# Block sums for the query products on GpSimd instead of VectorE

## The chip, the cores and the metric

The kernel runs on one core of a Trainium2 chip. A core has a matrix engine (TensorE, PE in the profile; its weight loads are listed apart as PEld), a vector engine (VectorE, DVE), a scalar engine (ScalarE, ACT), a programmable engine (GpSimd, POOL), and SyncE (SP), which here only issues DMAs. Every engine works through its own instruction stream in order, and waits on semaphores for the others. The metric is the time of one execution on the device, in microseconds.

## The reference

The inputs are `x` (2048 tokens of 512), key and value caches of 32 heads (2048 keys of 128), and weight matrices. All are bf16.

```
xn = layernorm(x)
q  = xn @ wq                                   # 2048 x 4096: 32 heads of 128
p  = softmax(q k^T / sqrt(128));  s = (p v) @ wo
h  = gelu(layernorm(xn) @ w1), its four quarters shifted by 1, -1, 2, -2 tokens
x1 = xn + h @ w2
g  = silu(x1 + gelu(layernorm(x1) @ w3) @ w4)
out = x + s * g
```

## The kernel before

**Stages.** The kernel first normalises the tokens, transposes them into `xnT` (features on the partitions, tokens along the free dimension), and runs most of the gated feed-forward part. From about 125 us it runs attention, with the rest of the feed-forward products mixed in up to about 191 us. Attention is one long loop over 128 units. A unit is one head and one block of 512 queries. Units go by groups of four heads, inside a group by the four query blocks, and inside a block by the four heads. A unit has 8 slots (`SPU`). In each slot TensorE makes the scores of 256 keys (`s_slot`), ScalarE exponentiates them into `pT` (line 436), and TensorE multiplies an earlier unit's `pT` by the values (`pv_run`, ten slots behind). Into the slots are woven the query projection of units to come, and the output projection of units that are done (`wo_slot`).

**VectorE's part in a unit.** It adds up the exponentials for the softmax's denominators: `add_first` (line 442), twice `add_next` (line 447), then `fold` (line 451) and `fold_last` (line 455). All of these read two tiles in SBUF. The sums are transposed by a DMA (`turn`), reduced (line 485), inverted (line 491), and spread by two more DMAs to `rb`. Then `norm` (line 509) scales the attention output from PSUM into `oT`. Lines 559 (first group) and 571 take the output projection out of its single PSUM bank (tag `xm`), which TensorE needs again for the next four products.

**The query projection.** Up to unit 15 the query tiles come from plain products of `xnT` and a head's weights. From unit 16 on, two heads at a time are projected with seven block products instead of eight (Strassen's scheme in Winograd's form). A pair's product is seen as 2 x 2 blocks: 256 tokens by 256 features, and 256 features by one head's 128 columns. The scheme needs sums of blocks:

- `x_sum(qt, i)`, line 356: four sums for each of the four query blocks, of 128 x 512 elements, made once (16 instructions). Sum 2 is written over a block of `xnT` itself, save for the last query block.
- `w_sum(h, i)`, line 365: four sums for each pair of heads from head 4 on, of 128 x 256 elements (14 pairs, 56 instructions). They lie in a tile `wc` with two buffers, so that a pair's sums can be written when the last product of the pair before the previous one has been read.

`product(v, k)` issues the seven products into one PSUM bank (tag `xa`). `q_take` (ScalarE, line 405) and `q_part` (VectorE, lines 413, 416, 418 and 421) combine them into the query tiles. Two of the products write into a half that `q_part` 1 and 2 (lines 416 and 418) must have read before.

**What sets the order.** The order is written out by hand: each instruction is pinned to program order on its engine, and `at(slot, fn)` places work at a slot. The token sums stand one per unit at slot 5 of units 10 to 25. The weight sums of a pair stand at slots 2 and 6 of two units, 4 or 2 units ahead of their group's (units 12 to 15, then every 16 units). The weights of a group's heads are loaded by SyncE's queue (`load_w`, line 164) in units 9 and 12 of the group before. The sums' tiles come from the pool `pS`, which opens in the place of the feed-forward's pool when the last feed-forward product has been issued.

```
for qt in range(QT):
    for i in range(4):
        at((10 + 4 * qt + i) * SPU + 5, lambda qt=qt, i=i: x_sum(qt, i))
for h in range(HG, H, 2):
    u = (h // HG) * QT * HG + (-4, -2)[h % HG // 2]
    for i in range(4):
        at((u + i // 2) * SPU + (2, 6)[i % 2], lambda h=h, i=i: w_sum(h, i))
```

GpSimd computes only some small operations for the layer norms (lines 194 and 205), all of them in the first 54 us.

Of the kernel before, what the change touches and what calls it, by code (L numbers as in the profile page):

```python
# [9 lines left out]
ALU = mybir.AluOpType  # L10
# [7 lines left out]
def kernel(  # L18
# [15 lines left out]
    nc = tc.nc  # L34
# [27 lines left out]
    pin = tc.keep_in_program_order  # L62
# [48 lines left out]
    def mm(out, lhsT, rhs, start, stop, **kw):  # L111
# [9 lines left out]
        out=ident[:], in0=diag[:], scalar1=0.0, scalar2=None, op0=ALU.is_equal))  # L121
# [219 lines left out]
    def x_block(qt, half, dcs):  # L341
        c = qt * 512 + 256 * half
        return xnT[:, dcs, c:c + 256]

    def x_sum(qt, i):
        if i == 2 and qt < QT - 1:
            out = x_block(qt, 1, LO)
        else:
            out = pS.tile([P, 2, 256], BF16, tag="xs", bufs=XS, name="xs")[:]
        a, b, op = (  # L350
            (x_block(qt, 1, LO), x_block(qt, 1, HI), ALU.add),
            (xs.get((qt, 0)), x_block(qt, 0, LO), ALU.subtract),
            (x_block(qt, 0, LO), x_block(qt, 1, LO), ALU.subtract),
            (x_block(qt, 0, HI), xs.get((qt, 1)), ALU.subtract),
        )[i]
        pin(nc.vector.tensor_tensor(out=out, in0=a, in1=b, op=op))
        xs[qt, i] = out

    def w_sum(h, i):
        if i == 0:  # L360
            wc[h] = pS.tile([P, 4, 2, Dh], BF16, tag="wc", bufs=2, name="wc")
        w, o = wc[h], [wc[h][:, k] for k in range(4)]
        b11, b12, b21, b22 = (wqs[h + j][:, d, :] for d in (LO, HI) for j in (0, 1))
        a, b = ((b12, b11), (b22, o[0]), (b22, b12), (b21, o[1]))[i]
        pin(nc.vector.tensor_tensor(out=o[i], in0=a, in1=b, op=ALU.subtract))

    def product(v, k):
        g, qt, hh = units[v]
# [313 lines left out]
    for jc in range(DC):  # L682
        b = BASE_J[jc]
# [153 lines left out]
    for g in range(NG - 1):  # L837
        b = (g * QT + QT - 1) * HG
# [62 lines left out]
    for v in pairs:  # L901
        a = (v - 2) * SPU
# [16 lines left out]
# [7 lines that stand above are left out]
# [108 lines left out]
    def pv_to(k):  # L1034
# [29 lines left out]
        out=diag[:], in0=diag[:], scalar1=0.0, scalar2=None, op0=ALU.is_equal))  # L1064
# [98 lines left out]
```

## Time and profile before

| what | value |
|---|---|
| median of 3 runs | 1236.7 us (1235.96 to 1236.73) |
| the profiled execution's own time | 1236.42 us |
| its span | 1234.6 us |
| TensorE busy | 1227.5 us (99%) |
| ScalarE busy | 1105.8 us (90%) |
| VectorE busy | 1030.1 us (83%) |
| GpSimd busy | 26.6 us (2%) |

The profile is of one execution. Busy time is the time in which an engine's instructions ran. The chain is the work that ended last, followed back from the last instruction to what released it. The waits tell how long an engine sat idle in front of an instruction, and which instruction of another engine released it, as total, number of times, and longest. A row of the timeline gives the start, the duration, the engine, the line, the operation, and the tiles (output, then inputs), with the idle time ahead of it and its releaser in brackets. A row by stretches gives the stretch, its length, the busy time and number of instructions, the granted clock of TensorE, the DMA share and the GB/s.

### The profile page before, as it was taken

How to read it: one execution, taken by the hardware profiler on the slowest of the kernel's cores; microseconds unless marked ns; L12 is line 12 of the kernel's file. 1: busy time of each engine (PE TensorE's matmuls, PEld its weight loads, DVE VectorE, ACT ScalarE, POOL GpSimd, SP SyncE). 2: the span in 40 equal slices, each digit the busy share in tenths (PEclk: the TensorE clock that was granted, in tenths of full speed). 3: DMA queues.
4: the chain of work that ended last, by engine and by line, in shares of the span. 5: the costliest groups of instructions: out<-in, count | busy, mean ns of one | idle time of the engine just before them, and what ended most of it. 6: DMA issues, size and time to landing. Idle time of an engine off the chain costs nothing.

```text
span 1234.6 us, 17534 instructions
## 1 busy us (share of the span) xinstructions
PE 1227.5 (99%) x6267; PEld 636.5 (52%) x6267; DVE 1030.1 (83%) x1647; ACT 1105.8 (90%) x1237; POOL 26.6 (2%) x75
## 2 busy tenths in 40 slices
PE   9999999999999999999999999999999999999998
PEld 6444444455555555555555555555555555555545
DVE  7712778899888888988889888888889999999997
ACT  6345999899999999999999999999999999999996
POOL 5300000000000000000000000000000000000000
PEclk9999999999999999999999999999999999999999
DMA  8661122664334423354243523543345424553342
GB/s 176 168 140 35 31 39 65 96 99 94 63 80 100 106 57 82 87 111 85 58 95 91 111 56 69 103 104 72 76 83 111 107 58 90 99 107 66 77 81 66
DMA packets 244056, 107.75 MB, mean 87 GB/s; under 512 B 194816, under 2 KB 227712, under 8 KB 243968
## 3 DMA queue, kind: packets, MB, share of 16 engines
q1 hardware_dynamic: 243408, 106.17, 41.5%
q8 instruction: 49, 0.80, 0.3%
q10 hardware_dynamic: 560, 0.46, 0.1%
q14 instruction: 39, 0.32, 0.1%
HBM read 67.50 MB, written 2.36 MB: 57 GB/s over the span
## 4 chain that ended last, share of the span: by engine, by line
PE 94%; DVE 3%; DMA 2%; ACT 1%; issue 0%; SPq 0%; DVEq 0%; ACTq 0%
PE ps_s L112 39%; PE ps_o L112 37%; PE ps_wo L112 8%; PE ps_q L112 8%; PE ps_m L112 2%; DMA tT<-acc 1%; DVE acc L447 1%; ACT pT L436 1%; DMA rb<-dr 0%; DMA xin<-in_A_x_dram 0%; DVE sm L485 0%; PE ps_oh L112 0%; DVE oT L509 0%; DVE acc L451 0%; DVE y L1025 0%
## 5 line engine op out<-in xcount | busy, mean ns | idle before, releaser
L436 ACT ACTIVATE pT<-ps_s 128x1024 bf16<-128x1024 f32 x1016 | 1016.2, 1025 | 56.8 <-PE ps_s L112 26.1
L112 PE MATMUL ps_s<-qT,kT 128*128 128x512 bf16 (+1 forms) x2064 | 609.3, 378 | 0.0
L112 PE MATMUL ps_o<-pT,vb 128*128 128x512 bf16 x1984 | 590.2, 379 | 0.0
L447 DVE TENSOR_TENSOR acc<-acc,pT 128x2048 bf16<-128x2048 bf16 x254 | 307.0, 1208 | 54.9 <-ACT pT L436 54.4
L112 PEld LDWEIGHTS <-kT 128*128 128x128 bf16 x2064 | 232.7, 113 | 151.3 <-issue 1.0
L112 PEld LDWEIGHTS <-vb 128*128 128x128 bf16 x1984 | 193.9, 98 | 216.6
L442 DVE TENSOR_TENSOR acc<-pT 128x2048 bf16<-128x2048 bf16 x127 | 155.4, 1224 | 38.4 <-ACT pT L436 35.5
L112 PE MATMUL ps_wo<-wo_h,oT 128*128 128x512 bf16 x496 | 186.3, 379 | 0.0
L451 DVE TENSOR_TENSOR acc<-acc 128x1024 bf16<-128x1024 bf16 x127 | 87.4, 688 | 2.5
L509 DVE TENSOR_TENSOR oT<-ps_o,rb 128x512 bf16<-128x512 f32 x127 | 86.6, 682 | 1.1 <-DMA rb<-dr 0.8
L485 DVE TENSOR_REDUCE sm<-tT 128x4 f32<-128x512 bf16 x124 | 83.9, 676 | 2.8 <-DMA tT<-acc 2.7
L112 PEld LDWEIGHTS <-oT 128*128 128x128 bf16 x528 | 51.4, 98 | 52.6 <-issue 0.6
L112 PEld LDWEIGHTS <-wc 128*128 128x128 bf16 x440 | 43.0, 98 | 54.1 <-issue 2.7
L571 DVE TENSOR_TENSOR sacc<-ps_wo,sacc 128x512 f32<-128x512 f32 x96 | 65.7, 684 | 0.0
L112 PEld LDWEIGHTS <-wq_h 128*128 128x128 bf16 x398 | 38.9, 98 | 46.3
L112 PE MATMUL ps_q<-xnT,wq_h 128*128 128x256 bf16 (+1 forms) x288 | 61.1, 298 | 0.4 <-DVE sacc L559 0.4
L421 DVE TENSOR_TENSOR qT<-ps_q,tq 128x512 bf16<-128x512 f32 x55 | 38.0, 692 | 23.3 <-PE ps_q L112 22.9
L455 DVE TENSOR_TENSOR acc<-acc 128x512 bf16<-128x512 bf16 x127 | 52.9, 417 | 0.5
L293 ACT ACTIVATE h2T<-ps_s 128x1024 bf16<-128x1024 f32 x28 | 28.6, 1023 | 25.9 <-PE ps_s L112 25.9
L112 PE MATMUL ps_s<-xn2T,w_sb 128*128 128x512 bf16 x224 | 48.8, 379 | 0.0
L112 PEld LDWEIGHTS <-w_sb 128*128 128x128 bf16 x368 | 33.5, 98 | 29.6
L112 PE MATMUL ps_q<-xs,wc 128*128 128x256 bf16 x246 | 47.0, 273 | 0.0
(102 smaller groups left out, 585.6 us busy)
## 6 DMA issues: line engine op xcount, KB each, us to landing
rb<-dr SPq DMA_DIRECT2D x127, 256.0 KB, 3.9
vb<-in_A_v_cache_dram SPq DMA_DIRECT2D x62, 256.0 KB, 3.0
wq_h<-in_A_wq_dram SPq DMA_DIRECT2D x32, 128.0 KB, 3.0
wo_h<-in_A_wo_dram SPq DMA_DIRECT2D x32, 128.0 KB, 2.5
w_sb<-in_B_w_dram SPq DMA_DIRECT2D x8, 256.0 KB, 5.0
kT<-in_A_k_cache_dram SPq DMA_TRANSPOSE x128, 2.8
xl<-in_A_x_dram SPq DMA_DIRECT2D x16, 128.0 KB, 3.0
dr<-rc SPq DMA_DIRECT2D x127, 2.0 KB, 1.4
```

What stands on the lines that cost most here:

```text
L112: pin(nc.tensor.matmul(out=out, lhsT=lhsT, rhs=rhs, start=start, stop=stop, **kw))
L293: pin(nc.scalar.activation(out=h2[c, f][:], in_=ps[:], func=ACT.Gelu_apprx_tanh))
L421: pin(nc.vector.tensor_tensor(out=s["q"][:, 1:3], in0=ps, in1=u.to_broadcast([P, 2] + list(u.shape[2:])), op=ALU.add))
L436: pin(nc.scalar.activation(out=s["pT"][-1][:, jj:jj + 2, :], in_=sps[:], func=ACT.Exp, scale=SCALE))
L442: pin(nc.vector.tensor_tensor(out=s["acc"][:], in0=s["pT"][0][:], in1=s["pT"][1][:], op=ALU.add))
L447: pin(nc.vector.tensor_tensor(out=a[:], in0=a[:], in1=st[u]["pT"][i][:], op=ALU.add))
L451: pin(nc.vector.tensor_tensor(out=a[:, 0:2, :], in0=a[:, 0:2, :], in1=a[:, 2:4, :], op=ALU.add))
L455: pin(nc.vector.tensor_tensor(out=a[:, 0, :], in0=a[:, 0, :], in1=a[:, 1, :], op=ALU.add))
L485: pin(nc.vector.tensor_reduce(out=sm[:], in_=s["tT"][:], axis=mybir.AxisListType.X, op=ALU.add))
L509: pin(nc.vector.tensor_tensor(out=to, in0=o, in1=rb, op=ALU.mult))
L571: pin(nc.vector.tensor_tensor(out=sa, in0=ps[:], in1=sa, op=ALU.add))
```

## The change

The two instructions that compute the block sums, `x_sum` and `w_sum`, are issued on GpSimd in place of VectorE. Their places in the program, tiles, operands and operations are the same. All other instructions are the same, and the order on TensorE and ScalarE is too; where TensorE waited for VectorE's sums, it waits for GpSimd's.

```
@@ def x_sum(qt, i):
-        pin(nc.vector.tensor_tensor(out=out, in0=a, in1=b, op=op))
+        pin(nc.gpsimd.tensor_tensor(out=out, in0=a, in1=b, op=op))
@@ def w_sum(h, i):
-        pin(nc.vector.tensor_tensor(out=o[i], in0=a, in1=b, op=ALU.subtract))
+        pin(nc.gpsimd.tensor_tensor(out=o[i], in0=a, in1=b, op=ALU.subtract))
```

## The prediction

> **What bounds the kernel now.** I read the page first (busy times, then the chain), next the waits of TensorE and VectorE, last the timeline beside the moved instructions.
>
> ```profile
> span 1234.6 us, 17534 instructions
> PE 1227.5 (99%) x6267; PEld 636.5 (52%) x6267; DVE 1030.1 (83%) x1647; ACT 1105.8 (90%) x1237; POOL 26.6 (2%) x75
> ...
> PE 94%; DVE 3%; DMA 2%; ACT 1%; issue 0%; SPq 0%; DVEq 0%; ACTq 0%
> ```
>
> TensorE (PE) is busy for 99% of the span and carries 94% of the chain that ended last. VectorE (DVE) is busy 83%, and GpSimd (POOL) 2%. So time that VectorE saves counts only where TensorE waits for it:
>
> ```profile
> PE ps_q L112 <- DVE qT L418: 1.4, 3, 1.0
> PE ps_q L112 <- DVE sacc L559: 0.4, 1, 0.4
> ```
>
> TensorE's waits for VectorE in the attention loop come to 1.4 + 0.4 us. VectorE follows TensorE with a margin, and the question is how large that is and what the new work on GpSimd does to it.
>
> **What is removed.** Grouped by line over the whole span, the 16 token sums (L356), then the 56 weight sums (L365):
>
> ```profile
> 0.00:1235.00 1235.00, 6.69 (x16) 1.00 0.42 87
> 0.00:1235.00 1235.00, 15.96 (x56) 1.00 0.42 87
> ```
>
> That is 6.69/16 = 0.42 us for a token sum and 15.96/56 = 0.285 us for a weight sum, 22.7 us in all. None of it lies on TensorE's path. The largest of the three waits shows why:
>
> ```profile
> 1057.50 0.29 DVE L365 TENSOR_TENSOR wc<-wq_h,wc 128x256 bf16<-128x256 bf16 x1
> 1060.30 0.69 DVE L485 TENSOR_REDUCE sm<-tT 128x4 f32<-128x512 bf16 x1 [1.32 <-DMA tT<-acc]
> 1064.23 0.38 PE L112 MATMUL ps_q<-xnT,wc 128*128 128x256 bf16 x2 [0.98 <-DVE qT L418]
> ```
>
> A weight sum stands ahead of it, but between the two VectorE waits 1.32 us for a DMA, so an earlier weight sum only lengthens that wait. I take the gain as 0, with 1.4 us as its upper end.
>
> **What is added: durations on GpSimd.** GpSimd has no such instruction before, so I bound it by its own rows (ns min/median/max, or busy and mean):
>
> ```profile
> L205 POOL TENSOR_SCALAR ve<-mv x30: 221/222/352, 6.1 to 53.3; 128x1 f32<-128x1 f32 x30
> L118 POOL IOTA diag<- 128x128 f32 x1 | 0.2, 242 | 0.4 <-POOLq L1147 0.4
> L1147 POOL MEMSET const-float32-0.0<- 128x1 f32 x1 | 0.1, 99 | 0.2 <-issue 0.2
> ```
>
> An operation on one element takes 0.22 us. The iota writes 128 elements in 242 ns against 99 ns for one, so about 1.1 ns per element of one stream. One stream's rate as the lower end: 0.22 + 512 x 1.1 ns = 0.79 us for a token sum and 0.50 for a weight sum. Two inputs fetched one after the other as the upper end: 1.35 and 0.79. No row separates them; I take the middle, 1.07 and 0.64, some 2.4 times VectorE's. (The Trainium skill, GPSIMD Engine Reference, section Elementwise — side-by-side cycle accounting, gives 4497 ns for 2048 fp32 elements; by its rate a token sum would be an estimated 1.12 us and a weight sum 0.56. No run here shows that yet.)
>
> **When they run.** GpSimd has nothing else to do after the layer norms, so the sums no longer run at VectorE's places (a token sum in each unit of 8 slots, from 217 to 347 us) but as soon as their data are there, in the order of the program. The pool of the sums opens when TensorE has read the last of the feed-forward tiles, and two token sums go at once. Then the first weight sum of heads 4 and 5 waits for its weights, and later that of heads 6 and 7 holds up the 15 instructions behind it (3 weight sums, 12 token sums):
>
> ```profile
> 191.04 0.38 PE L112 MATMUL ps_m<-w_sb,h2T 128*128 128x512 bf16 x1
> 207.13 1.12 SPq L164 DMA_DIRECT2D wq_h<-in_A_wq_dram  x2
> 236.02 0.39 SPq L164 DMA_DIRECT2D wq_h<-in_A_wq_dram  x1
> wq_h<-in_A_wq_dram SPq DMA_DIRECT2D x32, 128.0 KB, 3.0
> ```
>
> With 3.0 us from issue to landing, heads 4 and 5's weights are there at 207.13 + 1.12 + 3.0 = 211.3 us, and heads 6 and 7's at 236.02 + 0.39 + 3.0 = 239.4. At 211 us a short batch runs (4 weight and 2 token sums), and at 239 a burst starts: 4 x 0.64 + 12 x 1.07 = 15.4 us of GpSimd work, end to end, which before was spread out to 347 us. From head 8 on there are 12 batches of four weight sums, each released by TensorE's last read of the buffer.
>
> Being late is no danger. The first product that reads a combined weight comes at 249.6 us, and its sums (heads 4 and 5) start some 38 us sooner:
>
> ```profile
> L112 PE MATMUL ps_q<-xs,wc x246: 272/273/273, 249.6 to 1181.1; 128*128 128x256 bf16 x123
> ```
>
> **Contention, the term that decides.** The one place before where a GpSimd instruction is plainly lengthened beside VectorE is at 53 us:
>
> ```profile
> 51.94 0.57 POOL L194 TENSOR_TENSOR rs<-ve,nhalf 128x1 f32<-128x1 f32 x1
> 52.79 0.74 POOL L194 TENSOR_TENSOR rs<-ve,nhalf 128x1 f32<-128x1 f32 x1
> 53.65 0.58 POOL L194 TENSOR_TENSOR rs<-ve,nhalf 128x1 f32<-128x1 f32 x1
> 52.79 2.64 DVE L219 TENSOR_SCALAR xn<-xall,mv,rs 128x512 bf16<-128x512 bf16 x8
> ```
>
> The same GpSimd instruction takes 0.57 us ahead of the eight VectorE operations and 0.74 at their start, but 0.58 in their midst; the eight go at 2.64/8 = 0.33 us each. This is weak evidence that the engines hinder each other, in one direction, with a GpSimd operand of one element. Two ends: GpSimd gives way and VectorE is undisturbed (cost 0), or each holds the other off for whole instructions, turn about. I take the second, since the sums read 256 or 512 elements where this one reads one, and a resource that can stop GpSimd must be held by GpSimd when it comes first. (The Trainium skill, SBUF — State Buffer, section Who interferes with whom, states more than the row: a VectorE instruction with two SBUF inputs contends with a GpSimd instruction that reads SBUF, and whichever starts first holds the interface to its end. By that rule, with its durations above, the estimate is +5.6 us; by the row alone, which shows only GpSimd delayed, 0.)
>
> The VectorE instructions that would take turns are those with two SBUF inputs: L442, L447, L451, L455. In the burst they stand so before:
>
> ```profile
> 240.01 1.20 DVE L447 TENSOR_TENSOR acc<-acc,pT 128x2048 bf16<-128x2048 bf16 x1
> 241.24 0.69 DVE L451 TENSOR_TENSOR acc<-acc 128x1024 bf16<-128x1024 bf16 x1
> 241.96 0.43 DVE L455 TENSOR_TENSOR acc<-acc 128x512 bf16<-128x512 bf16 x1
> 242.51 1.22 DVE L442 TENSOR_TENSOR acc<-pT 128x2048 bf16<-128x2048 bf16 x1
> 244.77 1.23 DVE L447 TENSOR_TENSOR acc<-acc,pT 128x2048 bf16<-128x2048 bf16 x1 [0.71 <-ACT pT L436]
> ...
> 249.25 1.20 DVE L447 TENSOR_TENSOR acc<-acc,pT 128x2048 bf16<-128x2048 bf16 x1
> ...
> 254.97 0.68 DVE L559 COPY sacc<-ps_wo 128x512 f32<-128x512 f32 x1
> ...
> 259.02 0.42 DVE L418 TENSOR_TENSOR qT<-ps_q,tq 128x256 bf16<-128x256 f32 x1
> 256.05 0.38 PE L112 MATMUL ps_wo<-wo_h,oT 128*128 128x512 bf16 x1
> 260.37 0.38 PE L112 MATMUL ps_q<-xnT,wc 128*128 128x256 bf16 x2
> ```
>
> Turn about, with VectorE's own sums taken out: L447 240.0 to 241.2, token sum to 242.3, L451 to 243.0, weight sum to 243.6, L455 to 244.1, weight sum to 244.7, L442 to 245.9, token sum to 247.0, L447 to 248.2 (246.0 before). Over the next 2.6 us VectorE reads PSUM or one input, and GpSimd does three sums freely. Then L447 251.0 to 252.2, token sum 253.3, L451 254.0, token sum 255.0, L455 255.5, token sum 256.5, L442 257.7, token sum 258.8, L447 to 260.0. L559 ends at 260.7 instead of 255.65, and L418 at 265.5 instead of 259.44. TensorE needs L559 for its product at 256.05, a margin of 0.40 us, and L418 for that at 260.37, a margin of 0.93. The losses are 5.06 - 0.40 = 4.7 us and 6.05 - 0.93 = 5.1 us; being of one lag they don't add, and the larger counts: **+5.1 us**. With the lower durations the same steps give +2.7, with the upper +8.9, and then the short batch near 211 us may add what one token sum holds VectorE beyond the margin, 1.35 - 0.40 = 1.0: +9.9. With the middle durations I put it at 0: its six sums mostly fall beside VectorE work on PSUM.
>
> A later batch, turn about (before, around the release at 636.2 us):
>
> ```profile
> 635.71 1.23 DVE L442 TENSOR_TENSOR acc<-pT 128x2048 bf16<-128x2048 bf16 x1 [0.54 <-ACT pT L436]
> 638.08 1.21 DVE L447 TENSOR_TENSOR acc<-acc,pT 128x2048 bf16<-128x2048 bf16 x1
> 639.21 0.68 DVE L571 TENSOR_TENSOR sacc<-ps_wo,sacc 128x512 f32<-128x512 f32 x1
> 641.15 0.38 PE L112 MATMUL ps_wo<-wo_h,oT 128*128 128x512 bf16 x1
> ```
>
> L442 ends at 636.94, two weight sums fill the gap to 638.2, L447 starts 0.16 us late (0.44 with the upper duration), and the other two sums run beside L571 and its followers. The margin from L571's end (639.89) to TensorE's product at 641.15 is 1.26 us. Cost 0 for each of the 12; what hides it is VectorE's idle stretch and that margin.
>
> The sum against the profiled execution's own 1236.4 us: -0 + 5.1 + 0 = 1241.5. The median of the runs, 1236.7, lies 0.3 above; I forecast 1241.7 us.
>
> **Rivals.** (1) VectorE is undisturbed: GpSimd waits whenever VectorE works, as the row at 52.79 us shows, and the burst merely takes longer. For it: eight VectorE operations at their pace. Against it: nothing there could have held VectorE for long. The time is 1236.7, between 1235.3 (the whole gain of 1.4) and 1237.4 (a remainder of 0.7, one token sum caught running, 1.07, less the margin of 0.40).
> (2) Faster: VectorE undisturbed, and VectorE's relief removes TensorE's waits. The place is the three waits for L418 past 1000 us, the price 1.4 us; it decides only if also unrecorded gaps shrink and the sum passes 2.5 us. Against it stands the DMA wait of 1.32 us; 1234.
> (3) The weight sums are far slower than bounded. Past some 1.2 us each, two no longer fit before L447, and every one of the 12 batches loses about 1 us; token sums of 2.2 us carry the burst to about 17 (the loss grows by some 11 us per us of a token sum between my ends, (8.9 - 2.7)/(1.35 - 0.79)). 1236.7 + 17 + 12 = 1266.
>
> **How the numbers follow.** Forecast 0.55, with its own range 1239.4 to 1246.6 (1236.7 + 2.7 and + 9.9); rival 1 0.38; rival 2 0.03; rival 3 0.04. The range takes the forecast and rival 1: 1235.3 to 1246.6, leaving out 0.07 and the edges. About 0.2% (2.5 us) is what a measurement of this kernel can tell from no change; the forecast's low end lies just past it. Slower 0.55 + 0.04 = 0.59, the same 0.38, faster 0.03.
>
> **What would show it.** In the profile after: 72 rows of L356 and L365 on POOL, with means near 1.07 and 0.64 us or longer where they wait; a dense stretch from 239 to about 268 us; gaps of 0.6 to 1.1 us between L447, L451, L455 and L442 there; TensorE waiting for L559 and L418 near 255 to 270 us for 5 us, and no new waits after 300. It is wrong if VectorE's fold keeps its pace beside GpSimd's rows, if the burst starts elsewhere, or if TensorE loses time in each batch.

## The result and the profile after

The changed kernel takes 1240.59 us (median of 7 runs, 1239.58 to 1242.25), the kernel before 1236.29 us in the same series (7 runs, 1235.91 to 1236.91). The ratio is 1.0034, with a 95% interval of 1.0023 to 1.0046: slower by 4.3 us. The forecast was 1241.7 us, the range 1235.3 to 1246.6.

The profiled execution took 1240.59 us, its span is 1238.8. From the page of the changed kernel:

```profile
span 1238.8 us, 17434 instructions
PE 1223.0 (99%) x6149; PEld 637.3 (51%) x6267; DVE 1024.4 (83%) x1575; ACT 1106.1 (89%) x1237; POOL 108.7 (9%) x147
```

VectorE lost 72 instructions and 22.7 us of its own sums, yet its busy time fell by only 1030.1 - 1024.4 = 5.7 us: its other instructions became longer, by 17 us in all. (118 matmul records are missing from this trace, so TensorE's own busy time isn't compared.) GpSimd gained 108.7 - 26.6 = 82 us. Two of the groups of sums on GpSimd (ns min/median/max):

```profile
L356 POOL TENSOR_TENSOR xs<-xnT x5: 1154/2135/2139, 189.5 to 260.3; 128x512 bf16<-128x512 bf16 x5
L365 POOL TENSOR_TENSOR wc<-wq_h,wc x28: 658/667/1650, 212.9 to 1072.0; 128x256 bf16<-128x256 bf16 x28
```

The least is what the work itself takes, 1.15 us for a token sum and 0.66 for a weight sum. The rest, up to 2.14 and 1.65, is waiting inside an instruction, which the profile counts as busy. TensorE's waits for VectorE in the attention loop:

```profile
PE ps_wo L112 <- DVE sacc L559: 2.1, 1, 2.1
PE ps_q L112 <- DVE qT L418: 2.0, 5, 0.6
```

The first is new, and it is a single wait. This is the stretch before it, GpSimd first, then VectorE, then TensorE:

```profile
239.40 0.67 POOL L365 TENSOR_TENSOR wc<-wq_h 128x256 bf16<-128x256 bf16 x1 [22.01 <-DMA wq_h<-in_A_wq_dram]
240.03 2.13 POOL L356 TENSOR_TENSOR xs<-xnT 128x512 bf16<-128x512 bf16 x1
242.13 1.11 POOL L365 TENSOR_TENSOR wc<-wq_h,wc 128x256 bf16<-128x256 bf16 x1
...
262.42 1.60 POOL L356 TENSOR_TENSOR xs<-xnT,xs 128x512 bf16<-128x512 bf16 x1
```

```profile
239.91 1.25 DVE L447 TENSOR_TENSOR acc<-acc,pT 128x2048 bf16<-128x2048 bf16 x1
241.19 1.53 DVE L451 TENSOR_TENSOR acc<-acc 128x1024 bf16<-128x1024 bf16 x1
242.75 0.78 DVE L455 TENSOR_TENSOR acc<-acc 128x512 bf16<-128x512 bf16 x1
243.45 1.68 DVE L442 TENSOR_TENSOR acc<-pT 128x2048 bf16<-128x2048 bf16 x1
245.24 1.99 DVE L447 TENSOR_TENSOR acc<-acc,pT 128x2048 bf16<-128x2048 bf16 x1
...
253.85 2.17 DVE L442 TENSOR_TENSOR acc<-pT 128x2048 bf16<-128x2048 bf16 x1
...
258.04 0.68 DVE L559 COPY sacc<-ps_wo 128x512 f32<-128x512 f32 x1
...
262.93 0.41 DVE L418 TENSOR_TENSOR qT<-ps_q,tq 128x256 bf16<-128x256 f32 x1
```

```profile
258.77 0.38 PE L112 MATMUL ps_wo<-wo_h,oT 128*128 128x512 bf16 x1 [2.09 <-DVE sacc L559]
```

The two engines take turns. The token sum that starts at 240.03 lasts until 242.16, since VectorE's L447 runs until 241.16; L451, which starts behind L447, lasts 1.53 us instead of 0.69, since now the token sum has its turn. Behind a token sum L451 grew by 0.84, L442 (2.17 against 1.22) by 0.95 and L447 (1.99 against 1.22) by 0.77; behind a weight sum L455 grew by 0.36 and L442 (1.68) by 0.46. L559 reads PSUM and keeps its 0.68 us, but comes 3.1 us late (258.04 against 254.97), and TensorE waits 2.09 us for it.

Where the time went over the whole run can be read from the 1016 exponentials of line 436: the start of the n-th in the trace after, less that of the n-th before (us from the span's start in the trace before, us later in the trace after; a line where the difference moved):

```
120.41 0.10
248.39 0.34
256.89 2.73
261.21 3.03
278.38 3.54
961.21 4.11
1012.74 3.87
1065.08 3.53
1116.29 3.84
1222.41 4.11
```

3.4 of the 4.1 us arise between 240 and 280 us. The step of 0.5 us at 278 us is not a turn: the last sum on GpSimd ended at 264.0 us. VectorE waits there for the DMA that spreads the inverted sums (`rb`), first in the kernel before, then in the changed one, and TensorE after it:

```profile
273.10 0.69 DVE L509 TENSOR_TENSOR oT<-ps_o,rb 128x512 bf16<-128x512 f32 x1 [0.58 <-DMA rb<-dr]
277.15 0.69 DVE L509 TENSOR_TENSOR oT<-ps_o,rb 128x512 bf16<-128x512 f32 x1 [1.60 <-DMA rb<-dr]
281.08 0.38 PE L112 MATMUL ps_q<-xnT,wc 128*128 128x256 bf16 x2 [0.35 <-DVE qT L418]
```

Whether VectorE's lag made this DMA land late is not traced. The moves past 900 us add up to 0.6. They come at DMAs that land late, and the kernels e1_weights (0.55 at the start, 1.38 at 961 us, 1.59 at the end) and e3_none (0.21, 1.18, 0.62) have such moves at the same places, so I don't put them down to the change.

### The profile page after: what moved, and what is told of

Same layout as the page of the kernel before. It is cut to its first block, busy times and chain, and to the rows that moved or that the text cites. A ratio compares the mean times of both kernels' runs of the same rounds, so it can differ in the third digit from the quotient of the medians.

```text
span 1238.8 us, 17434 instructions
## 1 busy us (share of the span) xinstructions
PE 1223.0 (99%) x6149; PEld 637.3 (51%) x6267; DVE 1024.4 (83%) x1575; ACT 1106.1 (89%) x1237; POOL 108.7 (9%) x147
## 4 chain that ended last, share of the span: by engine, by line
PE 88%; DVE 7%; DMA 3%; ACT 1%; issue 1%; DVEq 0%; ACTq 0%
PE ps_s L112 37%; PE ps_o L112 34%; PE ps_q L112 8%; PE ps_wo L112 7%; PE ps_m L112 2%; DVE acc L447 2%; DMA rb<-dr 1%; ACT pT L436 1%; DMA tT<-acc 1%; DVE sm L485 1%; DVE acc L442 1%; DVE oT L509 1%; DVE acc L451 1%; DMA dr<-rc 0%; PE ps_warm L112 0%
## 5 line engine op out<-in xcount | busy, mean ns | idle before, releaser
L112 PE MATMUL ps_o<-pT,vb 128*128 128x512 bf16 x1906 | 573.1, 379 | 3.2
L447 DVE TENSOR_TENSOR acc<-acc,pT 128x2048 bf16<-128x2048 bf16 x254 | 310.2, 1221 | 56.4 <-ACT pT L436 55.8
L442 DVE TENSOR_TENSOR acc<-pT 128x2048 bf16<-128x2048 bf16 x127 | 157.5, 1240 | 43.5 <-ACT pT L436 43.4
L112 PE MATMUL ps_wo<-wo_h,oT 128*128 128x512 bf16 x475 | 178.4, 379 | 2.1 <-DVE sacc L559 2.1
L365 POOL TENSOR_TENSOR wc<-wq_h 128x256 bf16<-128x256 bf16 x28 | 35.7, 1276 | 800.2 <-PE ps_q L112 759.8
L451 DVE TENSOR_TENSOR acc<-acc 128x1024 bf16<-128x1024 bf16 x127 | 90.5, 713 | 2.5
L485 DVE TENSOR_REDUCE sm<-tT 128x4 f32<-128x512 bf16 x124 | 83.9, 676 | 3.2 <-DMA tT<-acc 2.9
L455 DVE TENSOR_TENSOR acc<-acc 128x512 bf16<-128x512 bf16 x127 | 55.0, 433 | 0.5
```

The source lines that it names most:

```text
L112: pin(nc.tensor.matmul(out=out, lhsT=lhsT, rhs=rhs, start=start, stop=stop, **kw))
L365: pin(nc.gpsimd.tensor_tensor(out=o[i], in0=a, in1=b, op=ALU.subtract))
L442: pin(nc.vector.tensor_tensor(out=s["acc"][:], in0=s["pT"][0][:], in1=s["pT"][1][:], op=ALU.add))
L447: pin(nc.vector.tensor_tensor(out=a[:], in0=a[:], in1=st[u]["pT"][i][:], op=ALU.add))
L451: pin(nc.vector.tensor_tensor(out=a[:, 0:2, :], in0=a[:, 0:2, :], in1=a[:, 2:4, :], op=ALU.add))
L455: pin(nc.vector.tensor_tensor(out=a[:, 0, :], in0=a[:, 0, :], in1=a[:, 1, :], op=ALU.add))
```

## The experiments

My theory, from the prediction: GpSimd's sums and those VectorE instructions that read two tiles in SBUF take turns, and the loss is VectorE's lag in the one dense stretch from 239 us, less the margin that TensorE has there. The rivals: the sums cost something wherever they run (the later batches too); what costs is the dependence on GpSimd, not its work; or any work of GpSimd on SBUF hinders VectorE. In each experiment the kernel before ran on the same chip. In its first series its median was 1236.79 us, in the second (from e5 on) 1236.62.

**Weight sums alone (e1_weights).** The token sums go back to VectorE:

```
@@ def x_sum(qt, i):
-        pin(nc.gpsimd.tensor_tensor(out=out, in0=a, in1=b, op=op))
+        pin(nc.vector.tensor_tensor(out=out, in0=a, in1=b, op=op))
```

> Only the 56 weight sums go to GpSimd, the 16 token sums stay on VectorE. If the loss is VectorE's lag in the one dense stretch of 12 token and 4 weight sums behind heads 6 and 7's weights, nearly all of it goes: 0 to 0.5 us over the kernel before. If the later batches of weight sums cost something each, or any work on GpSimd does, most of the 4.3 us stays: 3 us or more.

Measured: 1236.97 us, ratio 1.0005 (0.9996 to 1.0014). The 14 batches of weight sums cost nothing that can be measured; the loss belongs to the token sums or to their company.

**Token sums alone (e2_tokens).** The other half:

```
@@ def w_sum(h, i):
-        pin(nc.gpsimd.tensor_tensor(out=o[i], in0=a, in1=b, op=ALU.subtract))
+        pin(nc.vector.tensor_tensor(out=o[i], in0=a, in1=b, op=ALU.subtract))
```

> Only the 16 token sums go to GpSimd; with no weight sums between them that wait for weights, they run end to end from about 190 us, two to three units in which VectorE has more slack (2.0 us from line 509 to TensorE's next use, against 0.40 us at line 559 in the stretch at 256 us). If turns at the SBUF interface and the margin at the place decide, the lag of some 4 to 5 us loses 1 to 3 us. If the loss belongs to the units from 12 on alone, 0. If the token sums cost the same wherever they run, 3.5 to 4.3 us.

Measured: 1242.64 us, ratio 1.0042 (1.0028 to 1.0055). That is 3.5 to 6.8 us, more than I expected. The token sums do run end to end from 190 us, ten of them up to 207 us, and VectorE falls behind there. TensorE's rows:

```profile
207.12 0.90 PE L112 MATMUL ps_o<-pT,vb 128*128 128x512 bf16 x2 [1.98 <-DVE oT L509]
207.81 1.06 PE L112 MATMUL ps_s<-qT,kT 128*128 128x512 bf16 x2
208.67 1.06 PE L112 MATMUL ps_o<-pT,vb 128*128 128x512 bf16 x2
210.82 0.59 PE L112 MATMUL ps_q<-xnT,wq_h 128*128 128x512 bf16 x1 [1.09 <-DVE sacc L559]
```

The waits are 1.98 + 1.09 us, and 0.4 of that was there before: 2.7 us, within the 1 to 3 that I expected. But the pair of matmuls that takes 0.59 us elsewhere takes 1.06 behind the wait. By stretches (busy time and count of PE, PEld, DVE, ACT and POOL, then TensorE's granted clock, the DMA share and GB/s):

```profile
200.00:205.00 5.00, 4.95 (x23) 2.39 (x23) 4.90 (x5) 4.57 (x5) 4.92 (x4) 1.00 0.35 95
207.30:214.10 6.80, 5.71 (x14) 1.87 (x13) 4.50 (x7) 2.05 (x2) 0.05 (x1) 0.50 0.45 82
215.00:218.00 3.00, 3.00 (x15) 1.46 (x14) 2.17 (x3) 2.46 (x3) 3.00 (x3) 1.00 0.00 0
```

The granted clock was 0.50 for 6.8 us. On 5.71 us of busy time that costs an estimated 5.71 x 0.50 = 2.9 us, which I had not reckoned with. Waits and clock make 5.6 us, and by as much the exponentials of line 436 fall back here, between 205 and 209 us. But the clock is not the whole miss. Of the five runs, the two with a mean clock of 0.997 took 1243.46 and 1243.99 us; the three with 1.000 took 1240.97 to 1242.64, which is still 4.2 to 5.9 us over the kernel before, and what they lost beyond the waits isn't traced, as none of them has a profile. So by its time e2 doesn't refute the rival that the token sums cost the same wherever they run; that is left to e4.

**No sums at all (e3_none).** The products read plain blocks in place of the sums:

```
@@ def x_sum(qt, i):
+        xs[qt, i] = x_block(qt, 1, LO)         # no instruction
@@ def w_sum(h, i):
+        wc[h] = None                           # no instruction
@@ def product(v, k):
+        o = [b11, b21, b22, b11]
```

> No block sums at all: the products read the plain blocks of tokens and weights instead of the sums (the output is not the reference's), and TensorE's products are as many and as large. This measures what VectorE's relief of 22.7 us is worth by itself. By the prediction 0, at most 1.4 us faster than the kernel before. If it is more than 2 us faster, VectorE was worth relieving, and the loss on GpSimd is larger than the 4.3 us seen.

Measured: 1236.76 us, ratio 0.9998 (0.9989 to 1.0007). Without its 22.7 us of sums VectorE gains nothing that can be measured. So no placement of the sums can be expected to beat the kernel before by more than the 1.4 us that the interval leaves.

**Paced (e4_paced).** All sums on GpSimd, a unit's behind VectorE's second L447:

```
+    def paced(u, fn, *args):
+        if u not in paced_at:
+            paced_at.add(u)
+            pin(nc.gpsimd.tensor_copy(out=gate[:], in_=st[u]["acc"][:, 0, 0:1]))
+        fn(*args)
...
-            at((10 + 4 * qt + i) * SPU + 5, lambda qt=qt, i=i: x_sum(qt, i))
+            at((10 + 4 * qt + i) * SPU + 6, lambda qt=qt, i=i: paced(10 + 4 * qt + i, x_sum, qt, i))
...
-            at((u + i // 2) * SPU + (2, 6)[i % 2], lambda h=h, i=i: w_sum(h, i))
+            at((u + i // 2) * SPU + 6, lambda u=u, h=h, i=i: paced(u + i // 2, w_sum, h, i))
```

> All sums on GpSimd as in the change, but paced: ahead of the sums of a unit GpSimd copies one element of the unit's accumulator behind VectorE's second line 447, so that they run beside the 2.0 to 2.6 us in which VectorE reads PSUM or one input. The same GpSimd work, one unit at a time. If the dense stretch with its turns is the cause, the loss goes: 0 to 0.5 us over the kernel before. If GpSimd's work itself, its semaphores or TensorE's waits for GpSimd are, 3 to 5 us stay.

Measured: 1236.83 us, ratio 1.0000 (0.9991 to 1.0008). The whole loss is gone, with the same sums on the same engine. GpSimd in one unit, then VectorE in it (line 456 is the former 447, 460 the former 451):

```profile
237.94 0.19 POOL L373 COPY gate<-acc 128x1 bf16<-128x1 bf16 x1 [7.42 <-DVE acc L456]
238.08 1.17 POOL L357 TENSOR_TENSOR xnT<-xnT 128x512 bf16<-128x512 bf16 x1
239.21 0.67 POOL L366 TENSOR_TENSOR wc<-wq_h 128x256 bf16<-128x256 bf16 x1
239.96 0.67 POOL L366 TENSOR_TENSOR wc<-wq_h,wc 128x256 bf16<-128x256 bf16 x1
```

```profile
240.33 1.37 DVE L456 TENSOR_TENSOR acc<-acc,pT 128x2048 bf16<-128x2048 bf16 x1
241.74 0.69 DVE L460 TENSOR_TENSOR acc<-acc 128x1024 bf16<-128x1024 bf16 x1
```

The three sums take their least times beside VectorE's instructions that read PSUM or one input, and only the last touches the next L447 (1.37 in place of 1.20 us). In two later units the last weight sum still takes a turn (1.53 us at 257.52, 1.72 at 266.15), and the former L451 grows to 0.82 and 1.04 us; no wait of TensorE follows. So what costs is not the work on GpSimd as such, nor a single turn, but VectorE's lag from many turns one upon the other.

**The work without the dependence (e5_extra_tt).** VectorE computes all sums as before; GpSimd does 24 of the same kind (16 of a token sum's size, 8 of a weight sum's) into a spare tile. Of the edit, the spare tile's own lines are left out:

```
@@ def x_sum(qt, i):
         pin(nc.vector.tensor_tensor(out=out, in0=a, in1=b, op=op))
+        pin(nc.gpsimd.tensor_tensor(
+            out=xtra(2, 256), in0=x_block(qt, 0, LO), in1=x_block(qt, 0, HI), op=op))
@@ def w_sum(h, i):
         pin(nc.vector.tensor_tensor(out=o[i], in0=a, in1=b, op=ALU.subtract))
+        if h < 2 * HG:
+            if i == 0:
+                for j in (0, 1):
+                    pin(nc.gpsimd.tensor_copy(out=gate[:], in_=wqs[h + j][:, 0, 0:1]))
+            pin(nc.gpsimd.tensor_tensor(
+                out=xtra(2, Dh), in0=wqs[h][:, LO, :], in1=wqs[h + 1][:, LO, :], op=ALU.subtract))
```

> The kernel before with all its sums on VectorE, and in addition 24 instructions on GpSimd, as many, as large and in the same stretches as the change's up to 260 us: the same subtraction of two SBUF blocks, into a spare tile that nobody reads. If the loss is turns at the SBUF interface, it is there although nothing was moved, and larger than the change's by VectorE's own sums in the burst, which are still to be done (4 units of 0.42 + 0.57 us, some 2.3 units of them): 5 to 7 us over the kernel before, more if TensorE's granted clock drops after the wait. If the loss comes from dependences on GpSimd, 0.

Measured: 1247.12 us, ratio 1.0086 (1.0071 to 1.0101), 10.5 us slower. Nothing waits for GpSimd's results here, so the dependence is not the cause; the work is. TensorE waits twice, and its clock drops once:

```profile
250.69 0.59 PE L113 MATMUL ps_q<-xnT,wq_h 128*128 128x256 bf16 x2 [2.92 <-DVE qT L332]
265.01 0.38 PE L113 MATMUL ps_wo<-wo_h,oT 128*128 128x512 bf16 x1 [2.60 <-DVE sacc L574]
250.70:256.60 5.90, 5.90 (x16) 2.36 (x16) 5.83 (x8) 2.60 (x4) 5.59 (x5) 0.50 0.13 15
```

2.92 + 2.60 = 5.5 us of waits, in the expected 5 to 7, and an estimated 5.90 x 0.50 = 3.0 us of clock. These account for 8.5 us of the span's 9.4 more (1244.0 against 1234.6); the rest I have not traced.

**Writing only (e6_extra_iota).** The same places, with iotas in place of the subtractions:

```
+        pin(nc.gpsimd.iota(spare[0][:], pattern=[[-1, D]], base=0, channel_multiplier=1,
+                           allow_small_or_imprecise_dtypes=True))
```

> The same with instructions that read nothing: for each token sum two iotas, for each weight sum one, of 512 fp32 elements written to a spare tile (an estimated 0.67 us each by the iota row of the kernel before, 1.34 us in place of 1.16). If what is shared is the reading of SBUF, VectorE is undisturbed: 0 to 0.5 us over the kernel before, and lines 447, 451 and 455 keep 1.20, 0.69 and 0.42 us. If any work of GpSimd on SBUF holds VectorE off, 5 us or more.

Measured: 1236.93 us, ratio 1.0006 (0.9996 to 1.0015). GpSimd's rows and VectorE's (line 461 is the former 447, 465 the former 451, 469 the former 455):

```profile
240.41 0.56 POOL L361 IOTA spare<- 128x512 f32 x1
241.04 0.56 POOL L363 IOTA spare<- 128x512 f32 x1
240.05 1.20 DVE L461 TENSOR_TENSOR acc<-acc,pT 128x2048 bf16<-128x2048 bf16 x1
241.28 0.69 DVE L465 TENSOR_TENSOR acc<-acc 128x1024 bf16<-128x1024 bf16 x1
242.01 0.42 DVE L469 TENSOR_TENSOR acc<-acc 128x512 bf16<-128x512 bf16 x1
```

Neither engine is held off by the other. What the two engines contend for is reading SBUF; GpSimd's writing alone costs VectorE nothing.

**One input instead of two (e7_extra_copy).** In place of the subtractions, copies of one block:

```
-        pin(nc.gpsimd.tensor_tensor(
-            out=xtra(2, 256), in0=x_block(qt, 0, LO), in1=x_block(qt, 0, HI), op=op))
+        pin(nc.gpsimd.tensor_copy(out=xtra(2, 256), in_=x_block(qt, 0, LO)))
```

> The same with copies of one block, one SBUF input instead of two. If GpSimd holds VectorE off while it streams its inputs, a copy holds it off for about half as long (0.4 us against 0.84 for the token sum's size), and VectorE's lag in the burst stays near 2 to 3 us: 1.5 to 3.5 us over the kernel before. If the hold is a fixed price of each instruction, as with two inputs: 5 to 7 us. If only two inputs contend, 0.

Measured: 1238.45 us, ratio 1.0014 (1.0005 to 1.0024), 1.8 us slower. L451 (464 here) behind a copy of a token block:

```profile
241.37 0.98 DVE L464 TENSOR_TENSOR acc<-acc 128x1024 bf16<-128x1024 bf16 x1
```

0.98 - 0.69 = 0.29 us, against 0.84 behind a token sum; the largest growth behind copies is 0.41 (L447 at 255.04 us: 1.63 in place of 1.22), against 0.95. So the hold goes with what is read. A copy, 0.61 us by itself, holds VectorE off for somewhat less than half as long as a sum.

**More of it (e8_twice).** Nine token sums of the dense stretch are issued twice:

```
@@ def x_sum(qt, i):
-        pin(nc.gpsimd.tensor_tensor(out=out, in0=a, in1=b, op=op))
+        for _ in range(2 if qt > 0 and i != 2 else 1):
+            pin(nc.gpsimd.tensor_tensor(out=out, in0=a, in1=b, op=op))
```

> The change with 9 of the 12 token sums in the burst issued twice (the same values are written again). If VectorE's lag grows with each turn, by some 2.7 us per unit in which GpSimd does 7 to 8 token sums, 9 more cost about 3.3 us: 6.5 to 8.5 us over the kernel before, more if TensorE's clock drops. If VectorE's slack takes up what comes after the first units, or the loss is one late instruction, 4 to 5 us.

Measured: 1243.06 us, ratio 1.0056 (1.0041 to 1.0071), 6.4 us slower, just below the 6.5 to 8.5 that I expected. A part of it is clock again. TensorE's waits for L559 (560 here) in total, each of the two, and the stretch behind the first:

```profile
PE ps_wo L112 <- DVE sacc L560: 3.9, 2, 2.2
258.83 0.38 PE L112 MATMUL ps_wo<-wo_h,oT 128*128 128x512 bf16 x1 [2.21 <-DVE sacc L560]
279.58 0.38 PE L112 MATMUL ps_wo<-wo_h,oT 128*128 128x512 bf16 x1 [1.74 <-DVE sacc L560]
259.60:263.00 3.40, 3.31 (x10) 1.37 (x9) 3.37 (x6) 2.05 (x2) 3.32 (x3) 0.51 0.22 71
```

At a granted clock of 0.51, 3.31 us of busy time lose an estimated 3.31 x 0.49 = 1.6 us. The two runs with a mean clock of 1.000 took 1242.75 us each, 6.1 over the kernel before, the two with 0.999 took 1243.37 and 1243.96. The waits for this line grew from 2.1 us to 3.9, by a second one where the added sums run. So nine more sums cost some 1.8 us through turns, where I had 3.3: the direction is as expected, the rate was put too high.

## Why the prediction was right

**What bounds the kernel, and the gain of 0.** Right: without any sums the kernel is as fast as before (ratio 0.9998).

**Durations on GpSimd.** Right: 1.15 and 0.66 us undisturbed, against 1.07 and 0.64 taken from the middle of the bounds. No row had spoken for the middle, so that it fits is in part luck. The estimate from the figure in the Trainium skill, GPSIMD Engine Reference, section Elementwise — side-by-side cycle accounting (1.12 and 0.56) is too low for the smaller one.

**When they run.** Right: the burst starts at 239.40, as worked out, behind the weights of heads 6 and 7. It ends at 264 us, where I had 268, and pacing the same sums takes the loss away.

**Contention, turn about.** The mechanism is right, shown by e5 against e6 (reading against writing) and by e4 (the same work beside VectorE's other instructions). The sign that I named for it was wrong in form: there are no gaps between VectorE's instructions, the instructions themselves are longer. The rule of the Trainium skill, SBUF — State Buffer, section Who interferes with whom, agrees with the runs in which instructions contend: two SBUF inputs on VectorE, a read on GpSimd. Its hold to the end of the instruction is somewhat more than was measured here (0.77 to 0.95 us of a token sum's 1.15). The row at 53 us, on which the choice rested, was too weak for it; the choice could have gone wrong. Nor is that row the only one: in the first 26 us twelve rows of L205 on GpSimd take 0.29 to 0.35 us in place of 0.22, each starting beside a running L219 or L225 of VectorE, here L219 with L205, and an L205 without:

```profile
7.07 0.41 DVE L219 TENSOR_SCALAR xall<-xin,mv,rs 128x512 bf16<-128x512 bf16 x1
7.21 0.35 POOL L205 TENSOR_SCALAR ve<-mv 128x1 f32<-128x1 f32 x1 [0.18 <-DVE mv L203]
22.26 0.22 POOL L205 TENSOR_SCALAR ve<-mv 128x1 f32<-128x1 f32 x1 [2.55 <-DVE mv L203]
```

They too show only GpSimd delayed, but often and not once, and so spoke more strongly for some contention than the one row did.

**The term that was mis-sized** is the length of a turn, and with it the +5.1 us. I let each sum hold VectorE off for its whole duration, 1.07 and 0.64 us. Where VectorE's instructions had a whole sum to wait for, they grew by 0.77 to 0.95 us behind a token sum and by 0.36 to 0.46 behind a weight sum, 0.2 to 0.4 us less than the sums' own 1.15 and 0.66: a part of each sum ran beside VectorE. So L559 ended at 258.72, where I had 260.7, and TensorE waited 2.1 us, where I had 4.7. By 261 us the lag had cost 2.9 us (3.03 - 0.10) and not 5.1. Another 0.5 us came at 278 us, behind a late DMA that I had not listed. That the median of the runs still lies within 1.1 us of the forecast is in part luck: in the profiled run some 1.2 of its 4.1 us came from elsewhere than the turns.

**Later batches at 0.** Right: e1_weights is at 1.0005, and no wait there is new in kind. In the change's own batches it is GpSimd that waits, as here behind L447, which keeps its 1.22 us:

```profile
641.62 1.22 DVE L447 TENSOR_TENSOR acc<-acc,pT 128x2048 bf16<-128x2048 bf16 x1
641.71 1.65 POOL L365 TENSOR_TENSOR wc<-wq_h 128x256 bf16<-128x256 bf16 x1
```

**What I had not seen** is the clock. In the profiled run of the change TensorE's 2.09 us wait left the granted clock at 1.00. But of its seven runs the two with a mean clock of 0.998 took 1241.21 and 1242.25 us, the five with 1.000 took 1239.58 to 1240.69. A part of the median's distance, and most of its scatter, may be this; it was not traced, since only one run has a profile.

## What to carry to other kernels

Moving elementwise work from VectorE to an idle GpSimd can pay only if the engine that bounds the kernel waits for VectorE. A run without the work at all (e3) tells that first. If the work is moved, what counted here was not GpSimd's duration but which VectorE instructions stood beside it: those with two inputs in SBUF were held off by GpSimd's reads, those that read PSUM (L559, 0.68 us as before) or one input (L485, 0.67) were not. In VectorE's order the sums were also paced by the work around them. On an idle engine the same sums ran as soon as their data were there, all at once; tied to a point in each unit (e4) they cost nothing.

## What the runs showed of the hardware

- A GpSimd sum of 512 elements (1.15 us alone) adds 0.77 to 0.95 us to a VectorE instruction with two SBUF inputs that comes behind it (0.77 to L447, 0.84 to L451, 0.95 to L442), one of 256 (0.66 us) adds 0.36 to 0.46, a copy of 512 (0.61 us) adds 0.29 to 0.41, and an iota of 512, which reads nothing (0.56 us), adds 0. Both engines' rows show the waiting as busy time: a token sum behind L447 takes 2.13 us.
- TensorE's granted clock fell to 0.50 for 6.8 us (e2 and e5) and to 0.51 for 3.4 us (e8) at or behind waits of 1.98, 2.92 and 2.21 us, but not behind one of 2.09 us (the change; 1.00 from 259 to 264 us), nor behind one of 2.60 (e5, 265 us; 1.00 from 264 to 268 us). So a gap of this size sometimes costs, by estimate, nearly as much again as it lasts: 2.9 us behind 3.1 us of waits in e2, 3.0 behind 2.92 in e5, 1.6 behind 2.21 in e8. The Trainium skill, TensorE: Matmul & The Clock Gate, section What's actually happening, puts the drop after an idle window of some 3.4 us that runs free of the kernel's start; the drops here followed shorter waits, while that they come only sometimes agrees with a free-running window.
